# Windowed attention and a gated MLP on one core: V's scale through DRAM, and a pair's ten scores in one PE group

## The chip, the cores and the metric

One core of a Trainium2 chip runs the whole program: TensorE (PE), VectorE (DVE), ScalarE (ACT), GpSimd (POOL) and SyncE (SP), whose queue issues every transfer of this kernel. The metric is the device time of one execution in microseconds. Before the change the median of three runs is 649.65 us (648.05 to 651.03).

## The reference

Eight batches, eight heads, 576 positions, head dimension 64. Attention looks back over a window of 128 positions with a linear bias per head, and its output (8 x 64 = 512 channels) goes through a gated MLP with a spatial product.

```python
scores = scale * np.matmul(q, k.transpose(0, 1, 3, 2))
mask = (rel >= 0) & (rel < window)                  # window = 128
scores = np.where(mask, scores + bias[None], -1000000000.0)
attn = softmax(scores)                              # max taken off, sum + 1e-09
x = np.matmul(attn, v)                              # heads side by side: 512 channels

h = np.maximum(x @ w_in, 0.0)                       # 1024 channels: u and v
v_n = (v - mean(v)) / np.sqrt(var(v) + 1e-06)
v_s = np.einsum('ts,bsd->btd', w_spatial, v_n) + b_spatial[None, :, None]
out = (u * v_s) @ w_out
```

## The kernel before

**Attention.** Two heads make a pair, with 64 partitions each, so a batch has four pairs. The 576 queries of a pair are five tiles (four of 128, tile 4 of 64), and a tile of queries sees the keys of its own and of the tile before: 128, 256, 256, 256 and 192 columns. A pair goes through these steps, in `attention` (line 498 on):

- scores (L520): ten f32 matmuls in the 64-row shape, the two heads side by side in the array. They come in two PE groups (`PIECES`): tiles 0 to 3 in four PSUM banks with the tag `s`, and tile 4 in two banks of the same tag. A profile shows each f32 matmul as two records, so the groups are 16 and 4 records.
- DVE adds the bias and takes the row maximum (L531), ACT takes the exponential with its row sum (L537), ACT and DVE normalise into a high and a low f16 part, `pq` (L557, L562), and two transfers of SP transpose `pq` into `pt` (L568).
- V's scale: V is split into two f16 parts, which needs a power of two near the largest magnitude of the pair. ACT takes the sum of magnitudes of each partition into column 0 of `am` (L579); PE turns that column into a row (L583, in a bank with the tag `x`); DVE takes the maximum (L587, L588); two PE matmuls against constants bring it back to all 128 partitions, times 2^-12 and 2^-13/4096 (L593); DVE keeps the exponent bits (L599, L600). Then follow `vh` (L604 or L607) and `vl` (L611).
- P times V (L624): 42 small f16 matmuls into both banks with the tag `x`; ACT and DVE scale and split the result into the pair's `xt` (L633, L637).

**The gated MLP** of a batch is made of units, each one PSUM bank with the tag `m` (there are two): five V units (L689; L711 for the last 64 rows) of 512 columns, then eight U units (L741), eight spatial units (L762) and eight output units (L788) of 288 columns. V and U units take the four pairs one after another, three matmuls for each; output units go over four `gs` tiles in the same way. Behind a spatial unit DVE multiplies (L770) and splits (L776); the results of output units go to `o` and are stored by SP (L798). The weights are f32r parts, so a unit has 12 to 14 matmuls.

**The order.** `Plan` collects each step with its engine, a weight, a due time and what it reads and writes; tiles with a tag form rings of so many buffers. It then lists the steps by a simulated clock: on each engine the ready step with the earliest due time comes next. The engines run these lists in order. The scores, V's scale and P times V of batch b's pairs are thereby woven into the units of batch b - 1. SP's list holds loads, transposes and stores, and a transfer that waits there holds up those behind it.

The first batch and pair 0 of the second take another way (`raw_tile`, L430 to L484), without V's scale; the other 27 pairs take the way above.

## Time and profile before

| what | value |
|---|---|
| median of three runs | 649.65 us |
| profiled execution, its own time | 648.05 us |
| its span, first to last instruction | 646.3 us |
| PE busy | 619.0 us (96%) |
| DVE busy | 524.2 us (81%) |
| ACT busy | 430.9 us (67%) |
| granted TensorE clock, mean | 0.992 |
| share of PE in the chain that ended last | 79% |
| transfers, mean | 123 GB/s |

The profile is of the run with 648.05 us; 1.75 us of it lie outside the span. Matmuls are pipelined, so that the durations of their records overlap: 12 matmuls of 288 columns have records of some 0.3 us each, and start 0.13 us apart. A row of the timeline has the start, the length up to the end of the last record, engine, line, operation, tiles and shapes, and the number of instructions that it merges. The tiles' names in the profile: `qkraw` holds q and k, `s`, `x` and `m` are PSUM banks, `am` the scale, `one` the maximum, `ident` and `ones` constants.

### The profile page before, as it was taken

The numbers are of one execution on the slowest core, as the hardware profiler recorded it, in microseconds if no ns is written. First come the engines' busy times: TensorE is split into PE (matmuls) and PEld (weight loads), VectorE is DVE, ScalarE is ACT, GpSimd is POOL, SyncE is SP. The second block draws the span as 40 slices with busy tenths as digits, with TensorE's granted clock in tenths as the row PEclk, the third lists the DMA queues.
The fourth block names the chain that finished last, engine by engine and source line by source line (L and its number), as shares of the span: only waits on it lengthen the run. The fifth ranks groups of instructions, "written<-read, shape, count | busy, mean of one in ns | idle before, by whom it ended". The sixth has DMA issues, their size and how long they took to land.

```text
span 646.3 us, 14141 instructions
## 1 busy us (share of the span) xinstructions
PE 619.0 (96%) x5037; PEld 529.8 (82%) x5037; DVE 524.2 (81%) x1897; ACT 430.9 (67%) x1322; POOL 29.6 (5%) x53
## 2 busy tenths in 40 slices
PE   4879999999999999999999999999999999999997
PEld 2445688778899879988898979988898978988997
DVE  6999898999887979887887979887887979873632
ACT  4698675989585848686686848676686857662211
POOL 1000010000200010000100010000100010000100
PEclk9998799999999999999999999999999999999999
DMA  7903013799156863778165753858166751733001
GB/s 264 329 20 130 19 62 119 169 209 202 55 132 133 190 107 93 155 155 184 40 143 127 191 112 89 154 152 188 32 154 125 193 113 10 132 79 76 2 20 55
DMA packets 149291, 79.34 MB, mean 123 GB/s; under 512 B 128610, under 2 KB 139874, under 8 KB 149220
## 3 DMA queue, kind: packets, MB, share of 16 engines
q1 hardware_dynamic: 149220, 78.44, 51.8%
q8 instruction: 39, 0.64, 0.4%
q14 instruction: 32, 0.26, 0.1%
HBM read 37.13 MB, written 9.44 MB: 72 GB/s over the span
## 4 chain that ended last, share of the span: by engine, by line
PE 79%; DVE 17%; issue 1%; DMA 1%; ACT 1%; SPq 1%; ACTq 0%; DVEq 0%
PE m L762 16%; PE m L741 16%; PE m L788 14%; PE m L689 13%; PE s L520 8%; PE x L624 6%; DVE pq L562 4%; PE m L711 2%; DVE prob L436 2%; DVE prob L531 2%; DVE gs L298 1%; DMA pt<-in_qk_dram 1%; DVE prob L450 1%; DVE u L770 1%; DVE o L267 1%
## 5 line engine op out<-in xcount | busy, mean ns | idle before, releaser
L537 ACT ACTIVATE prob<-prob,stat 128x128 f32<-128x128 f32 (+1 forms) x270 | 125.4, 466 | 13.6 <-DVE stat L531 12.4
L762 PE MATMUL m<-wsp,vn 128*128 128x288 f32 x768 | 124.3, 299 | 0.7 <-DVE u L770 0.7
L788 PE MATMUL m<-gs,wout 128*128 128x288 f32 x768 | 113.5, 301 | 0.3 <-DVE gs L776 0.2
L762 PEld LDWEIGHTS m<-wsp,vn 128*128 128x128 f32 x768 | 107.5, 188 | 6.7 <-issue 1.9
L557 ACT ACTIVATE pq<-prob,stat 128x128 f16<-128x128 f32 x270 | 103.1, 464 | 12.7 <-ACT prob L537 10.2
L741 PE MATMUL m<-xt,win 128*128 128x288 f32 x768 | 111.6, 298 | 0.0
L788 PEld LDWEIGHTS m<-gs,wout 128*128 128x128 f32 x768 | 103.3, 188 | 7.2 <-issue 1.7
L562 DVE SCALAR_TENSOR_TENSOR pq<-prob,stat,pq 128x128 f16<-128x128 f32 x270 | 104.0, 437 | 4.3 <-ACT pq L557 3.7
L741 PEld LDWEIGHTS m<-xt,win 128*128 128x128 f32 x768 | 103.9, 188 | 4.1 <-issue 2.3
L689 PE MATMUL m<-win,xt 128*128 128x512 f32 x384 | 93.5, 396 | 1.7 <-DVE o L267 1.7
L531 DVE CUSTOM_DVE_ANT_0 prob<-s,tab 128x128 f32<-128x128 f32 (+1 forms) x270 | 89.2, 376 | 2.6 <-PE s L520 2.1
L689 PEld LDWEIGHTS m<-win,xt 128*128 128x128 f32 x384 | 71.5, 189 | 18.2 <-DVE o L267 2.8
L520 PE MATMUL s<-qkraw 64*128 64x256 f32 (+2 forms) x540 | 66.5, 360 | 1.5 <-DVE stat L531 1.3
L770 DVE TENSOR_TENSOR u<-m,u 128x288 f32<-128x288 f32 x64 | 28.9, 451 | 34.2 <-PE m L762 34.2
L520 PEld LDWEIGHTS s<-qkraw 64*128 64x128 f32 (+1 forms) x540 | 42.0, 175 | 16.2 <-issue 9.0
L659 POOL TENSOR_TENSOR st<-st,nhalf 128x1 f32<-128x1 f32 (+1 forms) x40 | 25.6, 640 | 560.4 <-DVE st L655 548.0
L537 ACT ACTIVATION_READ_ACCUMULATOR prob<-prob,stat 128x1 f32 x270 | 50.6, 187 | 0.0
L267 ACT COPY o<-m 128x288 f32<-128x288 f32 x37 | 14.6, 395 | 46.2 <-PE m L788 45.9
L624 PE MATMUL x<-pt,vh 128*64 128x256 f16 (+6 forms) x756 | 41.7, 229 | 0.0
L271 ACT ACTIVATE vt<-m 128x512 f32<-128x512 f32 x31 | 18.5, 598 | 33.0 <-DVE st L654 16.1
L637 DVE SCALAR_TENSOR_TENSOR xt<-x,am,xt 128x288 fp32r<-128x288 f32 x54 | 26.2, 507 | 17.1 <-ACT xt L633 17.0
L624 PEld LDWEIGHTS <-vh 128*64 128x64 f16 x756 | 31.7, 110 | 5.8 <-issue 3.5
(132 smaller groups left out, 820.7 us busy)
## 6 DMA issues: line engine op xcount, KB each, us to landing
qkraw<-in_qk_dram SPq DMA_DIRECT2D x28, 576.0 KB, 3.9
out_dram<-o SPq DMA_DIRECT2D x64, 144.0 KB, 2.0
vraw<-in_v_dram SPq DMA_DIRECT2D x28, 320.0 KB, 2.9
vn<-in_w_in_dram SPq DMA_DIRECT2D x6, 512.0 KB, 7.1
pt<-in_w_out_dram SPq DMA_DIRECT2D x4, 512.0 KB, 4.5
gs<-in_w_spT_dram SPq DMA_DIRECT2D x4, 288.0 KB, 5.0
xt<-in_w_in_dram SPq DMA_DIRECT2D x2, 512.0 KB, 6.8
qkraw<-in_qk_dram SPq DMA_DIRECT2D x3, 320.0 KB, 8.3
```

The lines of the kernel that those rows point to most:

```text
L520: nc.tensor.matmul(sc[k][j]()[:m, i, :k1 - k0], raw()[rows, 0, t * P:t * P + m], raw()[rows, 1, k0:k1], start=True, stop=True)
L531: nc.vector.tensor_tensor_reduce(pt(), sc()[:m, i, :n], tabs[h]()[:m, c0:c0 + n], -0.125, 3e38, ALU.add, ALU.min, st()[:m, NM, j, t:t + 1])
L537: nc.scalar.activation(pt(), pt(), AF.Exp, bias=st()[:m, NM, j, t:t + 1], scale=-1.0, accum_out=st()[:m, SM, j, t:t + 1])
L557: nc.scalar.activation(pq[j]()[:m, 0, cs], prob[j]()[:m, cs], AF.Copy, scale=st()[:m, RC, j, t:t + 1])
L562: nc.vector.scalar_tensor_tensor(pq[j]()[:m, 1, cs], prob[j]()[:m, cs], st()[:m, RC, j, t:t + 1], pq[j]()[:m, 0, cs], ALU.mult, ALU.subtract)
L624: nc.tensor.matmul(xp()[j * D:(j + 1) * D, x0:x0 + n], l()[:, kt, j * D:(j + 1) * D], rhs[:, o:o + n], start=j not in seen, stop=False, sk ...
L637: nc.vector.scalar_tensor_tensor(xt()[:, S + R + hf * HS:S + R + (hf + 1) * HS], xp()[:, :HS], am()[:, 6:7], xt()[:, qs].bitcast(F32), ALU ...
L689: nc.tensor.matmul(pt(), xt[c]()[:, X0[a] + t * P:X0[a] + (t + 1) * P], win()[:, c, w, DH:DF], start=(n == 0), stop=(n == 3 * NC_ - 1))
L741: nc.tensor.matmul(pt()[:, :HS], win()[:, c, w, d * P:(d + 1) * P], xt[c]()[:, X0[a] + hf * HS:X0[a] + (hf + 1) * HS], start=(n == 0), sto ...
L762: nc.tensor.matmul(pt()[:, :HS], l, r, start=(n == 0), stop=(n == len(ops) - 1))
L770: nc.vector.tensor_tensor(u(), pt()[:, :HS], u(), ALU.mult)
L788: nc.tensor.matmul(pt()[:, :HS], wout()[:, d, w, e * P:(e + 1) * P], gs[d]()[:, a, :], start=(n == 0), stop=(n == 3 * ND - 1))
```

## The change

**V's scale.** The column of magnitudes is written by SP to a tile in DRAM (`row`, 128 numbers) and read back by SP into all 128 partitions (`wide`, the front of the tile that `vl` will fill). DVE takes the maximum of each partition's 128 numbers, clamps it, keeps the exponent and multiplies by two constants (`powers`). The PE transpose, the two broadcasting matmuls and their bank are gone.

**The scores.** A new function `products` takes a list of groups. From batch index 2 on (`WHOLE = 2`) all ten scores of a pair form one PE group; tiles 0 to 3 stay in the four `s` banks, and tile 4 takes the two `x` banks that P times V also uses. DVE's steps of tile 4 get the earliest due times of the ten. The three pairs of batch index 1 keep two groups and `s` banks.

**The program's order.** `scores` and `attention` are now two functions, and the scores of a pair are recorded ahead of V's scale and P times V of the pair before it (`AHEAD = 1`), which sets the order in the rings of `s` and `x`.

```diff
+    AHEAD = 1
+    WHOLE = 2
...
+    dram = ctx.enter_context(tc.tile_pool(name="dram", bufs=2, space=bass.MemoryType.DRAM))
...
-    ones = fixed([1, 2 * P], BF16, "ones")
+    powers = fixed([P, 2], F32, "powers")
...
-    PIECES = (((0, 1), (2, 3)), ((4,),))
+    BANKS = (((0, 1), ("s", 4)), ((2, 3), ("s", 4)), ((4,), ("x", 2)))
...
+    def products(p, due, st, raw, RAWS, g, banks):
+        SM, NM, RC, TM = range(4)
+        sc = [[plan.buf(ps, *tag, [P, 2, 2 * P], F32) for _ in range(2)] for _, tag in banks]
+        span = [(k, i, t, min(P, S - t * P), max(0, (t - 1) * P), min(S, (t + 1) * P)) for k, (ts_, _) in enumerate(banks) for i, t in enumerate(ts_)]
+        def f():
+            for k, i, t, m, k0, k1 in span:
+                for j in range(2):
+                    rows = slice(j * D, (j + 1) * D)
+                    nc.tensor.matmul(sc[k][j]()[:m, i, :k1 - k0], raw()[rows, 0, t * P:t * P + m], raw()[rows, 1, k0:k1],
+                                     start=True, stop=True)
+        plan.add("PE", SWITCH + pe(*[4 * (x[5] - x[4]) for x in span]), due - 5000 + g * 3000, f, RAWS,
+                 [(sc[k][j], i) for k, i, *_ in span for j in range(2)])
...
+                d = due - 4500 + (t if len(banks) < 3 or t < NQ - 1 else -1) * 700 + j * 200
...
-        for g, banks in enumerate(PIECES):
+        for g, banks in enumerate((BANKS,) if b >= WHOLE else (BANKS[:2], ((BANKS[2][0], ("s", 4)),))):
+            products(p, due, st, raw, RAWS, g, banks)
...
+        return lambda: attention(p, due, vr, VRS, pts)
+    def attention(p, due, vr, VRS, pts):
...
-        def f():
-            nc.tensor.transpose(mp()[0:1, 0:P], am()[:, 0:1], ident())
-        def f():
-            nc.vector.tensor_reduce(one()[:, 0:1], mp()[0:1, 0:P], AX.X, ALU.max)
-            nc.vector.tensor_scalar(one()[:, 0:1], one()[:, 0:1], 2.0 ** -98, 2.0 ** 126, ALU.max, ALU.min)
-        def f():
-            for k in range(2):
-                nc.tensor.matmul(mp()[:, P + k:P + k + 1], ones()[:, k * P:(k + 1) * P], one()[:, 0:1], start=True, stop=True,
-                                 skip_group_check=True)
+        row = plan.buf(dram, "row", 2, [P, 1], F32)
+        wide = lambda: vl().rearrange("p a b -> p (a b)").bitcast(F32)[:, :P]
+        def f():
+            nc.sync.dma_start(row(), am()[:, 0:1])
+        plan.add("SP", 60, d + 1, f, [(am, 0)], [(row, 0)])
+        def f():
+            nc.sync.dma_start(wide(), row().rearrange("p o -> (p o)").partition_broadcast(P))
+        plan.add("SP", 300, d + 2, f, [(row, 0)], [(vl, 0)])
...
+            nc.vector.tensor_reduce(am()[:, 1:2], wide(), AX.X, ALU.max)
+            nc.vector.tensor_scalar(am()[:, 2:3], am()[:, 1:2], 2.0 ** -98, 2.0 ** 126, ALU.max, ALU.min)
+            nc.vector.tensor_scalar(am()[:, 2:3].bitcast(I32), am()[:, 2:3].bitcast(I32), bits, None, ALU.bitwise_and)
+            nc.vector.tensor_scalar(am()[:, 5:7], powers(), am()[:, 2:3], None, ALU.mult)
             nc.vector.tensor_scalar(am()[:, 5:6].bitcast(I32), am()[:, 5:6].bitcast(I32), bits, None, ALU.bitwise_xor)
...
+            todo.append((b, p, scores(b, p)))
+            if len(todo) > AHEAD:
+                rest(*todo.pop(0))
```

Where the order moves, three places matter. In the rows below, L numbers are those of the kernel that the rows are of; in the changed one the scores are L515, V units L700 and L722, U units L752, spatial units L773, output units L799 and P times V L635.

PE, in the middle of a batch, before: the scores of a pair, with U units.

```order
L689 MATMUL m<-win,xt 128x512 x24
L520 MATMUL s<-qkraw 128x128 x2
L520 MATMUL s<-qkraw 128x256 x6
L741 MATMUL m<-xt,win 128x288 x12
L583 MATMUL x<-ident,am 1x128
L741 MATMUL m<-xt,win 128x288 x12
L520 MATMUL s<-qkraw 64x192 x2
L593 LDWEIGHTS ones
L593 MATMUL x<-one,ones 128x1
```

PE at the same place with the change:

```order
L700 MATMUL m<-win,xt 128x512 x12
L722 MATMUL m<-win,xt 128x512 x8
L700 MATMUL m<-win,xt 128x512 x36
L515 MATMUL s<-qkraw 128x128 x2
L515 MATMUL s<-qkraw 128x256 x6
L515 MATMUL x<-qkraw 64x192 x2
L752 MATMUL m<-xt,win 128x288 x24
```

Tile 4's two matmuls stand directly behind the other eight and write to `x`; L583 and L593 are gone from between the units.

PE, at the turn from one batch's units to the next one's, before: the end of the batch's last P times V, two output units, and the first V unit.

```order
L624 MATMUL x<-pt,vl 64x64
L788 MATMUL m<-gs,wout 128x288 x24
L583 MATMUL x<-ident,am 1x128
L689 MATMUL m<-win,xt 128x512 x12
L593 LDWEIGHTS ones
L593 MATMUL x<-one,ones 128x1
```

PE at that turn with the change (the P times V is cut short):

```order
L515 MATMUL x<-qkraw 64x192 x2
L799 MATMUL m<-gs,wout 128x288 x48
L635 LDWEIGHTS vh
L635 MATMUL x<-pt,vh 64x256
...
L635 LDWEIGHTS vl
L635 MATMUL x<-pt,vl 64x64
L700 MATMUL m<-win,xt 128x512 x12
```

All four output units now stand ahead of P times V, and the first V unit directly behind it.

SP with the change, at the third scale that is made while a batch's units run (that of pair 0 of the next batch): `row` and `vl` are the two new transfers.

```order
L809 DMA out_dram<-o 128x288
L598 DMA row<-am 128x1
L809 DMA out_dram<-o 128x288
L602 DMA vl<-row 128x128
L578 DMA_TRANSPOSE pt<-pq_87 128x18x128
L578 DMA_TRANSPOSE pt<-pq_88 128x18x128
L414 DMA qkraw<-in_qk_dram 128x1152
```

DVE at the same scale with the change (L781 and L787 are the product and the split behind a spatial unit, L526 the maximum of scores):

```order
L781 TENSOR_TENSOR u<-m,u 128x288 x2
L607 TENSOR_REDUCE am<-vl 128x1
L608 TENSOR_SCALAR am<-am 128x1
L609 TENSOR_SCALAR am<-am 128x1
L610 TENSOR_SCALAR am<-powers,am 128x2
L611 TENSOR_SCALAR am<-am 128x1
L787 TENSOR_TENSOR gs<-u,gs 128x288 x2
L526 ISA prob_85,stat_89<-x,tab_71 64x192
```

On SP a pair's two transposes stand behind the second transfer, which waits for the first. On DVE the reduction, which waits for the second, stands between the products of the last two spatial units and their splits; behind these come the maxima of tile 4, which is the first tile that is read.

More of the change, by code (lines that the diff above doesn't have):

```diff
@@ L239, in f @@
             nc.vector.memset(ident(), 1.0)
-            nc.vector.memset(ones()[:, :P], 2.0 ** -12)
-            nc.vector.memset(ones()[:, P:], 2.0 ** -13 / PSC)
+            nc.vector.memset(powers()[:, 0:1], 2.0 ** -12)
+            nc.vector.memset(powers()[:, 1:2], 2.0 ** -13 / PSC)
             nc.vector.memset(nhalf(), -0.5)
             nc.vector.memset(rstat(), 1.0)
-        plan.add("DVE", dve(400), 500, f, (), [(ident, 0), (ones, 0), (nhalf, 0)] + [(rstat, k) for k in range(8)])
+        plan.add("DVE", dve(400), 500, f, (), [(ident, 0), (powers, 0), (nhalf, 0)] + [(rstat, k) for k in range(8)])
         def f():
@@ L492, in clear, with f @@
                      [k for a in range(2) for k in parts(pq[j], a * NB * P + OFF[NQ - 1], (a + 1) * NB * P)])
-    PIECES = (((0, 1), (2, 3)), ((4,),))
+    BANKS = (((0, 1), ("s", 4)), ((2, 3), ("s", 4)), ((4,), ("x", 2)))
     WINDOWS = (((0, 0, 256, 0), (1, 256, 160, 128), (2, 512, 32, 256)),
                ((1, 416, 96, 0), (2, 544, 224, 0), (3, 768, 192, 96), (4, 1024, 64, 224)))
-    def attention(b, p):
+    def products(p, due, st, raw, RAWS, g, banks):
[10 more added lines that the diff above has]
+                 [(sc[k][j], i) for k, i, *_ in span for j in range(2)])
+        for k, i, t, m, k0, k1 in span:
+            for j in range(2):
+                h, n, c0 = 2 * p + j, k1 - k0, P if t == 0 else 0
+                pt = lambda j=j, m=m, t=t, n=n: prob[j]()[:m, OFF[t]:OFF[t] + n]
+                d = due - 4500 + (t if len(banks) < 3 or t < NQ - 1 else -1) * 700 + j * 200
+                def f(sc=sc[k][j], pt=pt, i=i, j=j, h=h, t=t, m=m, n=n, c0=c0):
+                    nc.vector.tensor_tensor_reduce(pt(), sc()[:m, i, :n], tabs[h]()[:m, c0:c0 + n], -0.125, 3e38,
+                                                   ALU.add, ALU.min, st()[:m, NM, j, t:t + 1])
+                cols = parts(prob[j], OFF[t], OFF[t] + n)
+                plan.add("DVE", dve(n), d, f, [(sc[k][j], i), (tabs[h], 0)], cols + [(st, (NM, j, t))])
+                def f(pt=pt, j=j, t=t, m=m):
+                    nc.scalar.activation(pt(), pt(), AF.Exp, bias=st()[:m, NM, j, t:t + 1], scale=-1.0,
+                                         accum_out=st()[:m, SM, j, t:t + 1])
+                plan.add("ACT", act(n, 2), d, f, cols + [(st, (NM, j, t))], cols + [(st, (SM, j, t))])
@@ L502, in attention, with scores @@
+    def scores(b, p):
         due = FIRST + b * PERIOD - LEAD - (NP - 1 - p) * PERIOD // 4
@@ L510, in attention @@
                 raw_tile(b, p, t, raw, vr, xt, t % 4, due - 6000 + t * 1500)
[L511 to L539 removed]
+            return lambda: xt
+        for g, banks in enumerate((BANKS,) if b >= WHOLE else (BANKS[:2], ((BANKS[2][0], ("s", 4)),))):
+            products(p, due, st, raw, RAWS, g, banks)
         pts = []
@@ L830, in first, with rest @@
             win_weights(0, c, UDUE[c], w_u[c])
+    xts = []
+    def rest(b, p, f):
+        xts.append(f())
+        if p == NP - 1:
+            gated(b, [xts.pop(0) for _ in range(NP)])
     gated(0, x0, first)
+    todo = []
     for b in range(1, B):
-        xt = []
         for p in range(NP):
```

37 lines of the change are left out of this document (3 added, 34 removed).

## The prediction

> **What bounds the kernel now.** I read the page first (busy time, then the chain of work that ended last), and then three stretches of one batch each, from the first V unit (L689) of a batch to that of the next.
>
> ```profile
> PE 619.0 (96%) x5037; PEld 529.8 (82%) x5037; DVE 524.2 (81%) x1897; ACT 430.9 (67%) x1322; POOL 29.6 (5%) x53
> PE 79%; DVE 17%; issue 1%; DMA 1%; ACT 1%; SPq 1%; ACTq 0%; DVEq 0%
> 299.65:372.61 72.96, 72.53 (x620) 63.58 (x620) 61.04 (x224) 52.12 (x164) 3.17 (x5) 1.00 0.57 133
> 372.61:445.58 72.97, 72.53 (x620) 63.57 (x621) 61.04 (x224) 52.14 (x164) 3.17 (x5) 1.00 0.58 133
> ```
>
> In the last two rows the columns behind the length are PE, PEld, DVE, ACT and POOL, the granted clock, and the DMA share. A batch takes 72.96 us, PE is busy for 72.53 of it at full clock, DVE for 61.04. So PE sets the pace, and what is taken off PE is time, until DVE (11.9 us of slack) or a transfer steps in. A busy PE hides small losses, so I read the timeline from start to start: a block costs the distance from its first matmul to that of the next block.
>
> ```profile
> 314.74 1.79 PE L520 MATMUL s<-qkraw 64*128 64x128 f32 x16
> 316.46 1.85 PE L741 MATMUL m<-xt,win 128*128 128x288 f32 x12
> 318.16 0.27 PE L583 MATMUL x<-ident,am 128*1 128x128 f32 x1
> 318.18 1.84 PE L741 MATMUL m<-xt,win 128*128 128x288 f32 x12
> 319.96 0.54 PE L520 MATMUL s<-qkraw 64*64 64x192 f32 x4
> 320.43 0.20 PE L593 MATMUL x<-one,ones 1*128 1x1 bf16 x2
> ...
> 327.28 1.75 PE L741 MATMUL m<-xt,win 128*128 128x288 f32 x12
> 328.96 1.79 PE L520 MATMUL s<-qkraw 64*128 64x128 f32 x16
> 330.68 0.66 PE L762 MATMUL m<-wsp,vn 128*128 128x288 f32 x3
> ...
> 332.71 0.54 PE L520 MATMUL s<-qkraw 64*64 64x192 f32 x4
> 333.18 0.67 PE L762 MATMUL m<-wsp,vn 128*128 128x288 f32 x3
> ...
> 335.14 1.75 PE L741 MATMUL m<-xt,win 128*128 128x288 f32 x12
> 336.73 0.56 PE L762 MATMUL m<-wsp,vn 128*128 128x288 f32 x3
> ...
> 342.03 0.65 PE L762 MATMUL m<-wsp,vn 128*128 128x288 f32 x3
> ...
> 344.06 0.20 PE L593 MATMUL x<-one,ones 1*128 1x1 bf16 x2
> 344.19 1.86 PE L788 MATMUL m<-gs,wout 128*128 128x288 f32 x12
> 345.98 1.79 PE L520 MATMUL s<-qkraw 64*128 64x128 f32 x16
> ```
>
> The undisturbed unit is 335.14 to 336.73: 12 matmuls in 1.59 us, 0.1325 each, so 14 of L762 take 1.855. The same 12 take 1.68 ahead of scores (327.28 to 328.96): going into the 64-row shape costs 0.09.
>
> **What leaves PE.** The transpose of the maxima (L583): 318.18 to 319.96 is 1.78; less 1.59 and less 0.09 into the scores leaves 0.10, and its own step (318.16 to 318.18) is 0.02. I take **0.11 us**, far under the 0.27 of its record, which overlaps its neighbours.
>
> The two broadcasting matmuls (L593): the 14 matmuls from 342.03 to 344.06 take 2.03 instead of 1.855, of which 0.08 is the aftermath of a transpose just ahead and 0.09 the way in; their own step is 0.13 (344.06 to 344.19); the 12 behind them take 1.79 (344.19 to 345.98), 0.09 of it into scores and 0.11 aftermath. Together **0.33 us**. Behind tile 4's scores (319.96, 320.43) the way in and out is the scores' own, and only 0.13 goes; that is one pair in four.
>
> Tile 4's scores in a group of their own (332.71): the block ahead takes 2.03 (330.68 to 332.71), 0.09 of which is the way in; the block takes 0.47; the 14 behind it take 1.96 (333.18 to 335.14), 0.11 over: 0.67 in all. In the common group the work remains: the four tiles' 896 columns take 1.72 and these 192 take 0.47, so 1.78 ns per further column and 0.34 us. The merge saves **0.33 us**.
>
> [...]
>
> Two waits go with these instructions:
>
> ```profile
> 289.99 0.88 PE L520 MATMUL s<-qkraw 64*64 64x192 f32 x4
> 290.79 3.44 PE L788 MATMUL m<-gs,wout 128*128 128x288 f32 x24
> ...
> 298.94 0.27 PE L583 MATMUL x<-ident,am 128*1 128x128 f32 x1
> 299.65 0.73 PE L689 MATMUL m<-win,xt 128*128 128x512 f32 x2 [0.43 <-DVE o L267]
> ...
> 298.30 0.93 DVE L637 SCALAR_TENSOR_TENSOR xt<-x,am,xt 128x288 fp32r<-128x288 f32 x2
> 299.15 0.44 DVE L267 COPY o<-m 128x288 f32<-128x288 f32 x1
> ```
>
> Tile 4's group waits inside (0.80 to the next block, not 0.47): 0.33 once a batch from the third on (five times). And the first V unit starts 0.71 behind a transpose that costs 0.02 elsewhere: 0.68, four times (298.94, and at the same place of the next three batches), because its m bank is emptied by a DVE copy that stands behind the split of P times V. In the new order four output units and then P times V stand ahead of that V unit, so the bank it takes is emptied during P times V.
>
> **What moves, and what covers it.** At the batch's end P times V now stands directly ahead of the V units that need its pair.
>
> ```profile
> 304.69 2.91 PE L689 MATMUL m<-win,xt 128*128 128x512 f32 x12
> 307.53 0.41 PE L624 MATMUL x<-pt,vh 128*64 128x256 f16 x4
> ...
> 308.96 0.89 ACT L633 ACTIVATE xt<-x,am 128x288 fp32r<-128x288 f32 x2
> 309.04 5.78 PE L689 MATMUL m<-win,xt 128*128 128x512 f32 x24
> 309.70 0.50 DVE L637 SCALAR_TENSOR_TENSOR xt<-x,am,xt 128x288 fp32r<-128x288 f32 x1
> ```
>
> The first half of xt is there 310.20 - 309.04 = 1.16 us after PE is through with P times V. A V unit takes the pairs one after another, three matmuls each; the fourth pair is asked for by its tenth, after 9 x 0.237 (2.84 / 12) = 2.1 us. The cover holds by 0.9 us; gone, it costs up to 1.2 us a batch. In the same way a group of ten scores comes to tile 4, the one that waits for the x banks, 1.72 us after its start.
>
> **What is added.** DVE's five operations for four.
>
> ```profile
> L587 DVE TENSOR_REDUCE one<-x 1x1 bf16<-1x128 f32 x27 | 7.4, 273 | 0.0
> L599 DVE TENSOR_SCALAR am<-x 128x2 int32<-128x2 int32 x27 | 4.1, 154 | 12.3 <-PE x L593 12.3
> out_dram<-o SPq DMA_DIRECT2D x64, 144.0 KB, 2.0
> qkraw<-in_qk_dram SPq DMA_DIRECT2D x28, 576.0 KB, 3.9
> pt<-pq SPq DMA_TRANSPOSE x54, 4.7
> ```
>
> The reduction has the same 128 elements per partition (273 ns), the small ones 154 ns each; one more is 0.15 us a pair, 0.6 a batch, on an engine with 11.9 us to spare: nothing, as long as that slack lasts. SP issues two more transfers per pair, in a row: the second waits on SP for the first to land, and pq's transposes, loads and stores queue behind it. No row shows so small a transfer. From below it is the store of o, 2.0 us; from above a transpose, 4.7, if it runs into one; I take 2.0 to 2.5, nearest to the store, so 4 to 5 us from the maxima to DVE's reduction. DVE waits there only if the transfers are later than the order assumes; today it waits for PE at the same place, 12.3 us in all (the row of L599), without PE standing still for it.
>
> **The sum**, against the profiled execution's own 648.05 us (span 646.3 and 1.75 around it; the median of the runs shown is 649.65, 1.6 above):
> - transposes 27 x 0.11 = 3.0
> - broadcasts 20 x 0.33 + 7 x 0.13 = 7.5
> - merges, 24 pairs, 24 x 0.33 = 7.9
> - waits that go: about 4 x 0.68 and 5 x 0.33 = 4.4
>
> That is 22.8 us. New waits: DVE would be busy 61.7 of some 69.1 us, and the batch gets denser around two m banks.
>
> ```profile
> DVE am L599 <- PE x L593: 2.3, 2, 2.2
> ```
>
> From below they cost 0; from above 2.3 us a batch, as if all that DVE waits for the broadcast in the batch from 299.65 on (this row of its waits: 2.3 us in 2 waits) came out at PE. I take 0.7, nearer to 0 since the two covers hold in the rows; six batches make 4.2 us. The start, where PE waits for several things at once, I leave as it is. 648.05 - 22.8 + 4.2 = 629.5; the profiled execution being the fastest of its runs, I forecast **630**.
>
> **The rivals.**
>
> *DVE becomes the bound* (faster, by less). For: 84% busy, 89% in the shorter batch, and in-order. Against: its waits today are mostly for PE, and shrink with it. If its idle time falls only from 11.9 to 9.5 us, a batch takes 61.7 + 9.5 = 71.2: six batches gain 10.6, with the first batch's pairs (3 x 0.44 = 1.3) 12 us: 636.
>
> *The shared x banks couple two pairs* (faster, by less). P times V cannot start before tile 4 of the next pair's scores is read, nor these scores' last tile before ACT and DVE have emptied P times V. Against: in DVE's new order the two reads of tile 4 come first of the ten, and the 1.72 us above. If each of 24 groups waits 0.4 us, 9.6 us come back: 639.
>
> *The scale comes late and DVE stands still* (slower). One place: the scale behind the last spatial unit, where DVE has the reduction between two u products and the two gs splits that the next output units need. From the pair's Abs on ACT to there PE has three spatial units, 5.6 us, less the Abs itself; I estimate 5 us for both transfers. At 3.9 each, like the load of q and k, they take 7.8 and DVE waits 2.8 us; the scores (2.06) and nine matmuls (1.19) cover 3.25, but DVE's own 2.7 there (4 x 0.45, 0.9) use most of it: PE loses 2.3. At two of a batch's four scales, 14 in all, that is 32 us and 657. It decides from 22.8 / 27 = 0.84 us of lost PE per pair on. Against it: at the other places the order has more between them. [...]
>
> *The gain is swallowed* (no change). The planner's new order opens holes that eat all 22.8 us, at the start above all: 646 to 651. The order shows ten scores in one group and no L583 or L593, so the work itself does go.
>
> **Chances.** Forecast (622 to 634) 0.62; DVE's bound 0.18; x banks 0.08; late scale 0.06; swallowed 0.06. A measurement of this kernel tells about 0.5% from no change, 3.2 us. Faster: 0.62 + 0.18 + 0.08 and a part of the last, 0.89; same 0.05; slower 0.06. The range takes in the first three: from 622 (no new waits, 625, and the start's holes smaller too) to 642.
>
> **What would show it.** Right: a batch from V unit to V unit of 69 to 70.5 us, PE busy for nearly all of it; 20 records of scores in about 2.05 us start to start; the first V unit right behind P times V without a gap over 0.3 us; DVE waiting for row and vl transfers under 1 us each. Wrong in the price of switches: a batch without waits that is longer than 69.5. Late scale: DVE's reduction at the top of the waits, released by a transfer, and gaps of PE in output units. DVE's bound: PE gaps released by DVE copies and u products, and DVE above 90%.

## The result, and the profile after

The changed kernel takes **811.71 us** (median of 4 runs, 809.56 to 813.86) against 649.65 us for the kernel before in the same comparison (median of three; a fourth execution of it took 1167.1 us and isn't counted): a ratio of 1.2496, 95% interval 1.2438 to 1.2554. The forecast was 630. The page of the changed kernel, its first rows and the chain of work that ended last:

```profile
span 807.8 us, 14073 instructions
PE 657.9 (81%) x4956; PEld 573.0 (71%) x4956; DVE 530.9 (66%) x1922; ACT 437.4 (54%) x1324; POOL 30.0 (4%) x53
PEclk9988996979998789888898798988988999989999
PE 14%; DMA 7%; DVE 2%; ACT 2%; SPq 0%; issue 0%; ACTq 0%; DVEq 0%
```

81 instructions have left PE (5037 to 4956), and yet its records take 38.9 us more in all, since the granted clock falls (mean 0.898, before 0.992). DVE's busy time has hardly moved (524.2 to 530.9). No engine is near its limit. The chain could be followed back only to 595.25 us, so its shares can't be set beside those of before; of the 212.5 us that it covers, the 7% of DMA, nearly all of it the two new transfers, are some 59. Two batches in the middle, in the columns that the prediction explains:

```profile
376.94:472.87 95.93, 78.18 (x610) 70.29 (x608) 62.32 (x227) 52.88 (x163) 3.29 (x5) 0.88 0.53 100
472.87:568.95 96.08, 77.44 (x609) 69.48 (x608) 62.41 (x228) 52.89 (x163) 3.29 (x5) 0.89 0.54 102
```

A batch takes 96 us instead of 73. PE is idle for 18 of them, and its 610 instructions take 78 us. What was waited for, from the table of waits (engine, what it wanted to do, the releaser; us in total, times, longest), the third row from the same table of SP's queue; below them the reduction's row among the costliest groups:

```profile
DVE am L607 <- DMA vl<-row: 142.8, 26, 10.1
PE m L773 <- DVE u L781: 41.6, 7, 6.8
SPq L602 <- DMA row<-am: 156.9, 26, 8.4
L607 DVE TENSOR_REDUCE am<-vl 128x1 f32<-128x128 f32 x27 | 7.7, 286 | 142.8 <-DMA vl<-row 142.8
```

26 of the 27 reductions find their data missing, for 5.5 us in the mean. Before, DVE waited at this place for PE, 12.3 us in all. The rows of the transfers (size, then median us from issue to landing):

```profile
out_dram<-o SPq DMA_DIRECT2D x64, 144.0 KB, 4.0
vl<-row SPq DMA_DIRECT2D x27, 64.0 KB, 4.9
pt<-pq SPq DMA_TRANSPOSE x54, 5.4
row<-am SPq DMA_DIRECT2D x27, 0.5 KB, 8.8
```

The store of 512 bytes is the slowest of them, 8.8 us; the read takes 4.9. Together that is 13.7 us, where the prediction had 4 to 5. Stores of o are later too, 4.0 instead of 2.0. Such a median counts only transfers whose landing the profile can pair with their issue, and in the changed kernel these are few: 28 of the 64 stores of o, 9 of the 27 new stores and 13 of the 54 transposes. Where each transfer's completions are counted up to the next issue on the same semaphore, the store of o has 3.7 against 2.0 and the new store 8.5, but the transposes have 4.7 in both kernels; their 5.4 shows no delay.

One pair, from the timelines of SP, DVE and PE:

```profile
201.88 0.38 SPq L598 DMA_DIRECT2D row<-am  x1
209.03 0.32 SPq L602 DMA_DIRECT2D vl<-row  x1
209.44 6.85 SPq L578 DMA_TRANSPOSE pt<-pq  x2
...
213.38 0.29 DVE L607 TENSOR_REDUCE am<-vl 128x1 f32<-128x128 f32 x1 [4.73 <-DMA vl<-row]
216.07 0.45 DVE L781 TENSOR_TENSOR u<-m,u 128x288 f32<-128x288 f32 x1
...
210.22 1.74 PE L752 MATMUL m<-xt,win 128*128 128x288 f32 x12
216.57 0.97 PE L773 MATMUL m<-wsp,vn 128*128 128x288 f32 x3 [4.61 <-DVE u L781]
217.82 2.80 PE L773 MATMUL m<-wsp,vn 128*128 128x288 f32 x12
220.45 0.42 PE L773 MATMUL m<-r,l 128*128 128x288 f32 x2
```

SP stands behind its store from 201.88 to 209.03, DVE behind the read until 213.38. Queued behind DVE's reduction are the first steps of the next scores and then a u product; it is done at 216.52, and only then does PE, which ran out of work at 211.96, have an m bank. The clock is the second loss: behind the gap 12 matmuls take 2.63 us (217.82 to 220.45) instead of 1.59. Granted clock in that stretch, the sixth value behind the length:

```profile
216.57:220.71 4.14, 4.14 (x19) 4.14 (x20) 2.94 (x11) 4.01 (x17) 0.00 (x0) 0.59 0.97 260
```

### The profile page after: what moved, and what is told of

It reads as the page before. It is cut to its first block, busy times and chain, and to the rows that moved or that the text cites. A ratio compares the mean times of both kernels' runs of the same rounds, so it can differ in the third digit from the quotient of the medians.

```text
span 807.8 us, 14073 instructions
## 1 busy us (share of the span) xinstructions
PE 657.9 (81%) x4956; PEld 573.0 (71%) x4956; DVE 530.9 (66%) x1922; ACT 437.4 (54%) x1324; POOL 30.0 (4%) x53
## 5 line engine op out<-in xcount | busy, mean ns | idle before, releaser
L773 PE MATMUL m<-wsp,vn 128*128 128x288 f32 x768 | 138.3, 327 | 63.5 <-DVE u L781 41.6
L773 PEld LDWEIGHTS m<-wsp,vn 128*128 128x128 f32 x768 | 123.2, 215 | 67.7 <-DVE u L781 43.5
L799 PE MATMUL m<-gs,wout 128*128 128x288 f32 x768 | 126.2, 325 | 22.1 <-DVE gs L787 18.7
L532 ACT ACTIVATE prob<-prob,stat 128x256 f32<-128x256 f32 (+2 forms) x270 | 125.4, 467 | 33.7 <-DVE stat L526 33.5
L752 PE MATMUL m<-xt,win 128*128 128x288 f32 x768 | 119.4, 309 | 25.6 <-ACT vt L276 24.6
L799 PEld LDWEIGHTS m<-gs,wout 128*128 128x128 f32 x768 | 118.5, 214 | 28.7 <-DVE gs L787 20.3
L752 PEld LDWEIGHTS m<-xt,win 128*128 128x128 f32 x768 | 109.9, 198 | 31.6 <-ACT vt L276 25.8
L607 DVE TENSOR_REDUCE am<-vl 128x1 f32<-128x128 f32 x27 | 7.7, 286 | 142.8 <-DMA vl<-row 142.8
L700 PE MATMUL m<-win,xt 128*128 128x512 f32 x384 | 94.3, 401 | 5.9 <-DVE o L272 5.9
L700 PEld LDWEIGHTS m<-win,xt 128*128 128x128 f32 x384 | 73.4, 193 | 22.6 <-DVE o L272 6.1
L618 ACT ACTIVATE vh<-vraw,am 128x640 f16<-128x640 f32 x20 | 16.6, 828 | 133.7 <-DVE am L611 133.7
L526 DVE CUSTOM_DVE_ANT_0 prob<-s,tab 128x256 f32<-128x256 f32 (+2 forms) x222 | 75.6, 378 | 1.7 <-PE s L515 0.6
L781 DVE TENSOR_TENSOR u<-m,u 128x288 f32<-128x288 f32 x64 | 28.5, 451 | 43.2 <-PE m L773 43.1
L515 PE MATMUL s<-qkraw 64*128 64x256 f32 (+2 forms) x444 | 52.5, 371 | 3.0 <-DVE stat L526 3.0
L635 PE MATMUL x<-pt,vh 128*64 128x32 f16 (+6 forms) x756 | 46.8, 243 | 9.8 <-DVE stat L526 7.3
L532 ACT ACTIVATION_READ_ACCUMULATOR prob<-prob,stat 128x1 f32 (+1 forms) x270 | 51.1, 189 | 0.0
L635 PEld LDWEIGHTS <-vh 128*64 128x64 f16 x756 | 35.2, 118 | 15.6 <-issue 15.3
L515 PEld LDWEIGHTS s<-qkraw 64*128 64x128 f32 (+1 forms) x444 | 37.5, 190 | 12.2 <-issue 4.4
```

Source lines behind the costliest of these rows:

```text
L515: nc.tensor.matmul(sc[k][j]()[:m, i, :k1 - k0], raw()[rows, 0, t * P:t * P + m], raw()[rows, 1, k0:k1], start=True, stop=True)
L526: nc.vector.tensor_tensor_reduce(pt(), sc()[:m, i, :n], tabs[h]()[:m, c0:c0 + n], -0.125, 3e38, ALU.add, ALU.min, st()[:m, NM, j, t:t + 1])
L532: nc.scalar.activation(pt(), pt(), AF.Exp, bias=st()[:m, NM, j, t:t + 1], scale=-1.0, accum_out=st()[:m, SM, j, t:t + 1])
L635: nc.tensor.matmul(xp()[j * D:(j + 1) * D, x0:x0 + n], l()[:, kt, j * D:(j + 1) * D], rhs[:, o:o + n], start=j not in seen, stop=False, sk ...
L700: nc.tensor.matmul(pt(), xt[c]()[:, X0[a] + t * P:X0[a] + (t + 1) * P], win()[:, c, w, DH:DF], start=(n == 0), stop=(n == 3 * NC_ - 1))
L752: nc.tensor.matmul(pt()[:, :HS], win()[:, c, w, d * P:(d + 1) * P], xt[c]()[:, X0[a] + hf * HS:X0[a] + (hf + 1) * HS], start=(n == 0), sto ...
```

## The experiments

**The price of one small transfer.** The kernel before, with one more transfer per pair on SP's queue that nobody reads, in eight forms by turns.

```diff
+        kind = len(pairs) % 8
+        shape = ([P, 1], [P, 16], [P, P], [P, P], [1, P], [P, 1], [P, P], [P, P])[kind]
...
+            if kind == 0:
+                nc.sync.dma_start(to(), am()[:, 0:1])
+            elif kind == 1:
+                nc.sync.dma_start(to()[:, 0:1], am()[:, 0:1])
...
```

> The kernel before, with one extra small transfer per pair on SP that nothing reads, in eight forms by turns: the store of the column of maxima (128 x 4 B) packed into 512 B of DRAM, the same 64 B apart, the same 512 B apart, a store of 128 x 512 B, a store of 512 B from one partition, the column copied within SBUF (128 x 4 B), a broadcast read of 512 B into 128 partitions, a plain read of 128 x 512 B. Theory 1 (the late part is the confirmation of 128 writes into one short stretch of DRAM): the packed store lands after about 8 us, the spread stores and all others after 2 to 3 us. Theory 2 (4-byte writes to DRAM are slow wherever they go): all three 128 x 4 B stores take about 8 us, the 512-byte ones and the copy within SBUF 2 to 3. Theory 3 (the transfers of the changed kernel only waited in the rings behind other traffic): the packed store lands after 2 to 3 us here, as do all others. The time itself says little, since three forms hold up the f16 part of V.

651.0 us, beside 649.9 for the kernel before. The landing of each form, as the records of the trace's semaphores give it (issue to the last of its completions, 16 for all but the fifth form, which has 2; one value per transfer):

| form | us |
|---|---|
| 128 x 4 B into 512 B of DRAM (the change's store) | 8.6, 11.1, 8.75, 8.9 |
| 128 x 4 B, 64 B apart in DRAM | 7.2, 4.2, 4.2, 5.15 |
| 128 x 4 B, 512 B apart in DRAM | 4.2, 2.9, 1.9, 2.0 |
| 128 x 512 B to DRAM | 2.2, 4.55, 3.9 |
| 1 x 512 B to DRAM | 1.25 to 2.24 |
| 128 x 4 B within SBUF | 3.6, 4.8, 3.9 |
| 512 B of DRAM into all partitions | 3.2, 3.25, 3.3 |
| 128 x 512 B of DRAM into SBUF | 3.35, 3.6, 3.7 |

Neither the 512 bytes nor the 4-byte pieces make the store slow: 512 B apart the same pieces land in 1.9 to 4.2 us. Slow is to pack them into one stretch of 512 bytes: 8.6 to 11.1 us. Pieces 64 B apart lie between, 4.2 to 7.2; the one of 7.2 was issued 1.6 us behind a packed store. In the trace of the changed kernel, where no other 4-byte packets overlap them, the store's packets start 0.8 to 2.2 us after the issue and take 9 ns each; the 16 completions are spread out, mostly between 2 and 9 us. Why the shared stretch is slow no trace shows.

**Each half alone.** The merge and the new order, with V's scale left on PE; and the scale through DRAM alone, with the scores and the order of pairs as before.

```diff
 merge alone, against the changed kernel:
-            nc.sync.dma_start(row(), am()[:, 0:1])
-            nc.sync.dma_start(wide(), row().rearrange("p o -> (p o)").partition_broadcast(P))
+            nc.tensor.transpose(mp()[0:1, 0:P], am()[:, 0:1], ident())
...
 scale alone, against the changed kernel:
-    AHEAD = 1
-    WHOLE = 2
+    AHEAD = 0
+    WHOLE = 99
```

> The change without its scale: V's scale through PE as before, the ten scores of a pair in one group with tile 4 in the x banks, and the order with scores one pair ahead. Theory (PE sets the pace, a group of its own costs tile 4's scores 0.33 us, and the x banks' coupling is covered): 24 x 0.33 = 7.9 us and the wait of 0.33 inside five groups, 1.7, go, and some 1 to 2 come back: 641 us against 650, ratio 0.985 to 0.99. Rival (the x banks couple two pairs, and now three users share them): 650 to 660, with PE waits at the scores' records in x.

> The change without its merge: V's scale through DRAM, the scores in two groups and s banks and in the order of before. Theory (the two transfers take 8.8 and 4.9 us one after the other, and DVE, SP and then PE stand still behind them): 790 to 830 us, DVE's reduction waits for the transfer some 140 us in all. Rival (it takes the x banks and the new order to make the transfers late): under 700 us.

Merge alone: 648.03 us, ratio 0.9977 (0.9959 to 0.9994). Scale alone: 782.38, ratio 1.2070 (1.2006 to 1.2134). So the loss is the scale's; the order of the change makes it larger, 162 us over the kernel before instead of 133. Both expectations missed: the merge was to take 641 us, and the scale alone 790 to 830 with some 140 us of DVE's waits. The transfers of the scale alone, and DVE's waits for the read:

```profile
row<-am SPq DMA_DIRECT2D x27, 0.5 KB, 8.2
vl<-row SPq DMA_DIRECT2D x27, 64.0 KB, 4.9
...
DVE am L607 <- DMA vl<-row: 89.2, 22, 9.9
```

The merge alone gives less than its terms, because its order of pairs makes new waits: on the timeline of PE, P times V of one pair in each batch starts before `vl` is ready, and the U unit behind it waits for DVE.

```profile
320.43 0.41 PE L637 MATMUL x<-pt,vh 128*64 128x256 f16 x4
321.23 0.30 PE L637 MATMUL x<-pt,vl 128*64 128x256 f16 x2 [0.39 <-DVE vl L624]
...
323.46 0.79 PE L754 MATMUL m<-xt,win 128*128 128x288 f32 x4 [0.87 <-DVE u L276]
```

It is 3.03 us there from 320.43 to the next unit at 323.46, elsewhere 1.51. The ten scores take 2.19 us from start to start, 0.14 more than the predicted 2.05.

**The merge, with the scale's bank from the ring `s`** instead of `x`, on the guess that a third user of the x banks makes those waits:

```diff
-        mp = plan.buf(ps, "x", 2, [P, 512], F32)
+        mp = plan.buf(ps, "s", 4, [P, 512], F32)
```

> The merge alone with V's scale through PE, and the bank of that scale (the transposed maxima and the broadcast) taken from the four s banks instead of the two x banks. In the run of the merge alone P times V of one pair per batch stood still for 1.5 us within its 42 matmuls, where the scale's bank was a third user of the x banks. Theory (it is that third user): the gap goes, 6 x 1.5 = 9 us less than 648: about 639 us. Rival (it is tile 4's banks that P times V waits for): no change, 648.

664.48 us, ratio 1.0231 (1.0207 to 1.0256), where the guess gave 639. That place takes some 2 us instead of 3.03, but the scale's two PE steps and the U unit behind them lose 0.79, 1.25 and 1.14 us a batch, which then takes 75 us. So this run doesn't settle the guess; the kernel with a scale without transfers, further down, speaks against it.

**No transfer.** The changed kernel in its own order, without both transfers; the reduction takes a constant, so V's scale is left out.

```diff
-            nc.sync.dma_start(row(), am()[:, 0:1])
-            nc.sync.dma_start(wide(), row().rearrange("p o -> (p o)").partition_broadcast(P))
-            nc.vector.tensor_reduce(am()[:, 1:2], wide(), AX.X, ALU.max)
+            nc.vector.tensor_reduce(am()[:, 1:2], ident(), AX.X, ALU.max)
```

> The changed kernel without both transfers, in the same order: DVE's reduction reads a constant tile. It leaves out V's own scale (a constant one is used). It shows what the rest of the change brings. By the prediction's sum: 625 to 634 us. With what the run of the merge alone showed in place of it (the block of ten scores takes 2.19 us, not 2.05, so a merge saves 0.20 and not 0.33: 24 x 0.13 = 3.1 us less): 630 to 640 us. Rival (the x banks stop P times V here too, 1.5 us a batch and more): 640 to 650.

636.91 us, ratio 0.9794 (0.9777 to 0.9811). One batch, and PE's wait at the first V unit of a batch:

```profile
302.53:372.77 70.24, 69.54 (x609) 62.77 (x608) 61.87 (x228) 52.69 (x164) 3.29 (x5) 1.00 0.61 138
...
PE m L700 <- DVE o L272: 3.6, 5, 0.8
```

All of the change but the two transfers works: 13.2 us faster than 650.09. The transfers cost 811.7 - 636.9 = **174.8 us**. (The kernels were measured in several comparisons, in which the kernel before lay between 648.3 and 650.1 us; a difference of 2 us across them says nothing.)

**The waits one by one.** Three kernels in the changed order. DVE's reduction takes a constant, with both transfers as they are. Or the read takes a row of the input V, so that it doesn't wait for the store, which is still made. Or the read goes to a tile that nobody uses and DVE takes a constant, so that SP alone waits for the store. In none of them is V's scale the pair's.

```diff
 DVE's reduction free:
-            nc.vector.tensor_reduce(am()[:, 1:2], wide(), AX.X, ALU.max)
+            nc.vector.tensor_reduce(am()[:, 1:2], ident(), AX.X, ALU.max)
...
 store not waited for:
-            nc.sync.dma_start(wide(), row().rearrange("p o -> (p o)").partition_broadcast(P))
+            nc.sync.dma_start(wide(), v[0, 0][0, 0, :].partition_broadcast(P))
...
 only SP waits:
-            nc.sync.dma_start(wide(), row().rearrange("p o -> (p o)").partition_broadcast(P))
+            nc.sync.dma_start(side(), row().rearrange("p o -> (p o)").partition_broadcast(P))
```

> The changed kernel, instruction for instruction, but DVE's reduction reads a constant tile instead of what the broadcast read brings: both transfers still run and SP still waits for the store, DVE waits for neither. It leaves out V's own scale (a constant one is used). Theory (DVE, an in-order engine, stands before its reduction, 143 us in all, and PE behind it): nearly all is back, 635 to 660 us. Rival (SP, held 157 us behind the store, lets transposes, loads and stores come late, and they stop PE by themselves): above 700 us.

> The changed kernel, but the broadcast read takes 512 B of the input in place of the stored maxima: the store runs and nobody waits for it, DVE still waits for the read. It leaves out V's own scale (the maximum of other numbers of V is used). Theory (the store takes 8.8 of 13.7 us, and the list of steps has room for some 5): 640 to 670 us, and DVE waits under 1.5 us per pair. Rival (3 to 5 us of the read are enough to stop DVE): above 700 us.

> The changed kernel, but the broadcast read lands in a tile of its own that nobody reads, and DVE's reduction reads a constant tile (in the run where only the reduction was freed, DVE still waited 82 us for the same transfer at the low part of V, which overwrites its target). It leaves out V's own scale (a constant one is used). SP still waits for the store. Theory A (what SP holds up behind the store is enough): 690 to 750 us, with PE and DVE waiting for transposes and for stores of o. Theory B (DVE's and ACT's wait for the scale is what stops PE; SP's hold is covered): 637 to 655 us.

| kernel | us | ratio |
|---|---|---|
| DVE's reduction free | 751.23 | 1.1559 (1.1527 to 1.1592) |
| store not waited for | 722.55 | 1.1118 (1.1093 to 1.1143) |
| only SP waits | 731.41 | 1.1263 (1.1228 to 1.1299) |

The first is no clean cut: the read lands in the front of `vl`, so DVE waits for it one step later, 81.9 us in all. Waits of the second and the third:

```profile
DVE am L607 <- DMA vl<-in_v_dram: 65.4, 25, 7.0
vl<-in_v_dram SPq DMA_DIRECT2D x27, 64.0 KB, 7.6
```

```profile
DVE o L272 <- DMA out_dram<-o: 54.3, 14, 7.5
PE x L635 <- DMA pt<-pq: 24.9, 11, 9.3
```

No single waiter holds the loss: each wait that is taken away leaves 70 to 100 us over the kernel before. In the second a read of the input, which waits for nothing, lands after 7.6 us when it stands behind the store (3.2 to 3.3 by itself, above). In the third DVE and PE wait for stores of o and transposes, which the change doesn't touch.

**Planned for.** The changed kernel, its order made as if the store took 6.6 us and the read 2.7 us more, with Abs, store and read due 12 us earlier.

```diff
-        plan.add("SP", 60, d + 1, f, [(am, 0)], [(row, 0)])
+        plan.add("SP", 60, d0 + 1, f, [(am, 0)], [(row, 0)], lag=6600)     # d0 = d - 12000, for Abs too
-        plan.add("SP", 300, d + 2, f, [(row, 0)], [(vl, 0)])
+        plan.add("SP", 300, d0 + 2, f, [(row, 0)], [(vl, 0)], lag=2700)
```

> The changed kernel, with the list of steps made for what the two transfers took: 6.6 and 2.7 us are added to the planner's delay of the store and of the broadcast read, and the sum of magnitudes and both transfers are due 12 us earlier. Theory (the work on PE is less by 22.8 us, and the time was lost because the reduction stood in DVE's list, and the read in SP's, 9 us too early): 625 to 640 us, DVE waits under 1 us per pair for the transfer. Rival (so small a store also holds up the transfers around it, or SP has no room for it): over 660 us, with SP still waiting for the store and the transposes late.

726.35 us, ratio 1.1173 (1.1120 to 1.1225). DVE's wait for the read is gone, and the expectation of 625 to 640 still fell; its rival, over 660 with the transposes late, came (6.1 us by the median of the page, 4.7 before). Waits of DVE and of SP's queue:

```profile
DVE o L273 <- DMA out_dram<-o: 40.1, 9, 10.2
SPq L604 <- DMA row<-am: 32.1, 6, 8.3
```

**POOL's queue** for both transfers, in the changed order:

```diff
-            nc.sync.dma_start(row(), am()[:, 0:1])
+            nc.gpsimd.dma_start(row(), am()[:, 0:1])
```

and the read likewise.

> The changed kernel with both transfers issued from POOL's queue instead of SP's, in the same places of the order. SP no longer waits for the store. Theory A (SP's hold is most of the loss): under 720 us. Theory C (the slow confirmation of the store delays every transfer that follows it on the same 16 engines, whoever issued it; in the run where nobody waited for the store, the read behind it took 7.6 us instead of 3.2): above 760 us, the transfers of SP still land late (stores of o 4 us instead of 2.0), and DVE waits as long as in the changed kernel.

801.32 us, ratio 1.2347 (1.2318 to 1.2376). SP no longer stands behind the store, but POOL does (95.3 us in 11 waits), the store is about as slow from here (8.1 us), the transposes of SP's queue land after 5.9 us by the median of the page, which counts only those that it can pair with their issue, and DVE still waits 105.5 us for the read (142.8 in the changed kernel). The stores of o, expected at 4 us, have 2.3:

```profile
pt<-pq SPq DMA_TRANSPOSE x54, 5.9
row<-am POOLq DMA_DIRECT2D x27, 0.5 KB, 8.1
...
DVE am L607 <- DMA vl<-row: 105.5, 22, 10.5
```

**The store alone, the read alone, and the store 512 B apart.** After these runs it was open how the loss divides between the slow confirmation, what it does to transfers behind it, and a wait for any read in this order. Four kernels: the kernel without transfers, with the packed store added that nobody reads or waits for (V's scale left out); the changed kernel without the store, the read taking a row of the input V (not the pair's scale); and the changed kernel with the store's 4-byte pieces 512 B apart, once in its own order and once planned for. In these two the read takes the first partition's sum alone, so the maximum over partitions is left out.

```diff
 512 B apart:
-            nc.sync.dma_start(row(), am()[:, 0:1])
+            nc.sync.dma_start(apart()[:, 0:1], am()[:, 0:1])               # apart: [P, P] in DRAM
-            nc.sync.dma_start(wide(), row().rearrange("p o -> (p o)").partition_broadcast(P))
+            nc.sync.dma_start(wide(), apart()[0:1, :].rearrange("o f -> (o f)").partition_broadcast(P))
```

> The order of the kernel without the two transfers (636.9), and the store of the 128 sums alone, which nobody waits for; there is no read, and the reduction takes a constant, so V's scale is left out. Theory (a slow store costs only through those who wait for it): 636 to 645, transposes 4.7 to 5.0 us and stores of o 2.0 to 2.4. Rival (each transfer behind it is confirmed late as well): transposes above 5.5 us or stores of o above 2.8, waits of DVE for out_dram<-o and of PE for pt<-pq as in the run in which SP alone waited, time above 655.

> The changed kernel without the store; the broadcast read takes a row of the input V, and DVE waits for it as in the changed kernel, so V's scale is not the pair's. Against the run with the store not awaited (722.6, read 7.6 us): theory (the store in front of it makes the read late) read 3.2 to 3.8 us, time 640 to 665. Rival (the read alone is late in this order, and DVE's wait for it is the price): read above 5 us, time above 700.

> The changed kernel in its own order; the 128 sums are stored 512 B apart (first column of a 128x128 tile in DRAM), and the read takes that tile's first row, so V's scale comes from the first partition's sum alone: a part of the computation is left out. Theory (the price is that 128 writes of 4 B go into one stretch of 512 B): the store is confirmed 2 to 4 us after its issue instead of 8.8 and the read lands in 3 to 4, so DVE waits for the read under 50 us in all instead of 143, and the time is 640 to 690. Rival (any two small transfers in a row on SP in this order cost this, wherever they write): store above 6 us, time above 722, the time of the run in which the store was not awaited.

> The store 512 B apart as in the run above (scale from the first partition alone), and the order made with 1.8 and 2.0 us more for the two transfers and with Abs, store and read due 12 us earlier. Theory (with a store that is confirmed early the order can cover both transfers): DVE's wait for the read under 10 us in all, time 636 to 650, near the kernel without transfers. Rival (moving the transfers on SP disturbs transposes and stores as it did with the packed store, 726): above 690.

| kernel | us | ratio |
|---|---|---|
| no transfer | 636.91 | 0.9794 (0.9777 to 0.9811) |
| read alone, DVE waits for it | 640.87 | 0.9878 (0.9852 to 0.9904) |
| store 512 B apart, then the read | 644.27 | 0.9933 (0.9907 to 0.9958) |
| store 512 B apart, planned for | 648.66 | 0.9991 (0.9973 to 1.0008) |
| packed store alone, nobody waits | 683.32 | 1.0549 (1.0516 to 1.0582) |
| packed store, only SP waits | 731.41 | 1.1263 (1.1228 to 1.1299) |
| packed store and read: the change | 811.71 | 1.2496 (1.2438 to 1.2554) |

With the pieces 512 B apart, and the same instructions in the same order (beside one transfer that fills the tile at the start), the changed kernel is **no longer slower** than before: it is 0.7% faster, a small gain that the interval still sets apart from none. Its transfers, a batch in the middle, and DVE's wait:

```profile
apart<-am SPq DMA_DIRECT2D x27, 0.5 KB, 2.0
vl<-apart SPq DMA_DIRECT2D x27, 64.0 KB, 2.9
...
377.69:448.21 70.52, 69.79 (x609) 62.82 (x608) 61.89 (x228) 52.67 (x163) 3.29 (x5) 1.00 0.64 139
...
DVE am L610 <- DMA vl<-apart: 8.8, 7, 2.9
```

So 811.7 - 644.3 = 167.4 of the 174.8 us hang on the addresses of the store; a prompt store and the read together cost 7.4. The read changes a little with it: it needs one stored piece instead of 128, and lands after 2.9 us instead of 4.9; no run has the read of all 128 behind a prompt store. The read by itself costs 4.0, the order covers it nearly everywhere (DVE waits for it 5.2 us in all, in four waits). It lands after 3.3 us there:

```profile
vl<-in_v_dram SPq DMA_DIRECT2D x27, 64.0 KB, 3.3
```

That is the kernel with the unawaited store (722.55, read 7.6) less that store: a packed store that nobody waits for makes the read behind it 4.3 us later and the kernel 81.7 us longer.

The packed store alone costs 46.4 us by the medians although nobody waits for it. Its five runs spread from 672.02 to 685.10 us, the two lowest, 672.02 and 678.82, below the interval in the table; so the cost is 35 to 48. The expectation had the theory that a slow store costs only through those who wait; it fell. On SP's timeline, in the chain of waits, and among the waits of that kernel:

```profile
593.41 0.53 SPq L598 DMA_DIRECT2D row<-am  x1
595.31 10.34 SPq L809 DMA_DIRECT2D out_dram<-o  x3
...
595.31 9.40 DMA out_dram<-o
...
DVE o L272 <- DMA out_dram<-o: 35.1, 10, 10.6
```

A store of o that is issued 1.9 us behind the packed store lands 9.4 us later, at 604.71; without the packed store the median is 2.1. Its own 128 packets of 1152 B have all ended within 1.4 us of the issue, so what is late is the confirmation and not the data. The first of its 16 completions comes 0.7 us after the last of the packed store's. DVE waits for it with the next copy of o, and has ten such waits in all; without the packed store there is none. The trace of the changed kernel shows the same: five stores of o that are issued 0.4 to 0.5 us behind the packed store (one at 350.98) land after 8.3 to 11.0 us, four of them with the 128 packets ended by 1.4. In these four the first completion comes 0.4 to 2.5 us before the packed store's last. So the slow confirmation reaches transfers behind the store; the traces show the lateness, not what orders the completions.

Planned for, the kernel with the prompt store has no wait at the reduction left:

```profile
L612 DVE TENSOR_REDUCE am<-vl 128x1 f32<-128x128 f32 x27 | 7.3, 271 | 0.0
```

It is still no faster than before: the other order loses more elsewhere than the 8.8 us of waits that it saves. Two batches take 144.2 us there instead of 141.0; which waits make that up wasn't worked out. That it came in within its expected 636 to 650 is no merit of the plan.

**A scale without transfers.** One matmul against a 128 x 128 constant gives every partition the sum over all partitions, times 2^-12; DVE reads it from PSUM. The scale is then a power of two near the sum, instead of near the maximum, of the 128 sums. Once with the merge and the new order, once on the kernel before.

```diff
-            nc.sync.dma_start(row(), am()[:, 0:1])
-            nc.sync.dma_start(wide(), row().rearrange("p o -> (p o)").partition_broadcast(P))
+            nc.tensor.matmul(mp()[:, 0:1], ones(), am()[:, 0:1], start=True, stop=True, skip_group_check=True)
-            nc.vector.tensor_reduce(am()[:, 1:2], wide(), AX.X, ALU.max)
-            nc.vector.tensor_scalar(am()[:, 2:3], am()[:, 1:2], 2.0 ** -98, 2.0 ** 126, ALU.max, ALU.min)
+            nc.vector.tensor_scalar(am()[:, 2:3], mp()[:, 0:1], 2.0 ** -110, 2.0 ** 114, ALU.max, ALU.min)
```

> The merge and the order of the change, with V's scale by one PE matmul and no transfer: a 128 x 128 tile of constants times the column gives every partition the sum of all 128 (in place of their maximum; both bound V's largest magnitude, and the scale is a power of two that is undone behind P times V). Transpose, broadcast and the single-partition reduction are gone. Theory (PE sets the pace; the run without transfers took 637 us, and the matmul has the array's full shape, so some 0.1 us): 637 to 643 us. Rival (its bank is a third user of the x banks, 1.5 us a batch as in the merge alone): 646 to 650.

> The kernel before with nothing changed but V's scale by that one matmul: the scores in two groups, s banks, the order of before. By the terms of the prediction's sum: broadcasts 7.5 us and, of the transposes' 3.0, some 1.5 go, and the wait of the first V unit behind the transpose, 0.68 four times, may go too: 638 to 642 us. Rival (another wait takes their place): 645 to 650.

With the merge **634.50 us, ratio 0.9777 (0.9758 to 0.9795)**, faster than both kernels and under the 637 to 643 expected; on the kernel before 642.12, ratio 0.9895 (0.9876 to 0.9913), at the upper edge of its 638 to 642. A batch of the first:

```profile
368.52:439.07 70.55, 70.55 (x617) 63.73 (x616) 63.62 (x234) 49.48 (x155) 2.78 (x5) 1.00 0.60 138
```

PE is busy for all of it: this comes near to the kernel that the prediction had in mind, without the transfers. The scale's bank is here again a third user of the x banks, and in the middle batches P times V takes 1.51 us in nearly every pair, 1.85 at most. So a third user need not make the wait of the merge alone; here it holds its bank for one step of PE instead of two with DVE between them.

## Why the prediction was wrong

**What bounds the kernel, and what leaves PE: right but for two terms.** Without the transfers a batch takes 70.24 us, within the 69 to 70.5 that the prediction named, and the kernel 13.2 us less than before. It had 22.8 less 4.2, 18.6.

Two terms of that sum were mis-sized. The merge had 0.33 us for each pair; the ten scores take 2.19 us, so it is 0.33 - 0.14 = about 0.2, or 4.6 for 24 pairs instead of 7.9. And the wait of the first V unit for DVE's copy of o was to go (4 x 0.68); 3.6 us in five waits are still there, since P times V ahead of it didn't cover the copy. That the prediction charged 0.7 per batch for new waits makes up for part of this by luck: it is the old wait, not a new one. Taken by the batch, transposes 0.44, broadcasts 1.12, merges 0.8 and tile 4's wait 0.33 make 2.69; measured are 72.96 - 70.24 = 2.72.

**The covers, as far as the runs show them: right.** In the kernel without transfers no V unit waits for `xt`, and the scores wait 2.9 us in all for an emptied bank, in the first batch. There the rival of the x banks didn't come, and neither did DVE's bound: the batch of 70.55 us, in the kernel with the scale by one matmul, has DVE at 63.62, 90%, and PE idle at no point.

**What is added: this is the step that failed.** "No row shows so small a transfer. From below it is the store of o, 2.0 us; from above a transpose, 4.7 ...; I take 2.0 to 2.5, nearest to the store". The store took 8.8 and the read 4.9. The store of o was the wrong neighbour: it moves 144 KB in runs of 1152 bytes, this one 128 pieces of 4 bytes into one stretch, and no row of the trace before had that form. The bound from above was no bound. Where the pieces are 512 B apart, the two take 2.0 and 2.9 us, close to what the prediction took, and the kernel is at 644: the step failed by the addresses, not by the count of bytes or transfers. Even with a prompt store the forecast would have been low by 14 us, mostly by the two terms above and the 7.4 us that two prompt transfers cost.

**Where the cost falls: named as a rival, priced too low.** "The scale comes late and DVE stands still" gave the mechanism (reduction at the top of DVE's waits, released by a transfer, PE without m banks) and also what would show it; those rows are the ones above, though the gaps stand at spatial units more than at output units. It took 3.9 us for each transfer, 14 of 27 scales, and 0.06 for its chance. At 13.7 us for both, the same working gives DVE 13.7 - 5 = 8.7 us of wait and PE 8.7 - 0.55 = about 8 at a late scale, where the change costs 174.8 / 27 = 6.5 in the mean of all.

What it missed altogether is that a slow store reaches those who don't use it. It counted the queue of SP behind the store, but held the durations of all other transfers fixed. The packed store alone, awaited by nobody, costs 35 to 48 us; with the read and SP's wait 94; with DVE's wait 175. Part of each is the clock, which the prediction left out as well (granted in the mean 0.965, 0.944 and 0.898 in these three, 0.987 without transfers): in the changed kernel PE is busy for 657.9 us with the same 4956 matmuls that take 605.5 without transfers, 52 us more, at a granted clock of 0.898 in the mean. How much of these 52 lies on the path and how much beside other waits wasn't separated.

## What to carry to other kernels

Price a transfer by its pieces and where they land, not by its bytes or by the nearest row of another form: 128 pieces of 4 B into one stretch of 512 B of DRAM took 8.8 us here, the same pieces 512 B apart 2.0. Where no row has that form, measure it in a side transfer that nobody waits for, and leave the bound open above until then. And ask of a slow store what is issued behind it: taking its waiters away (683 to 751 us), planning for it (726) or moving it to another queue (801) didn't take the cost away here, where the kernel without transfers takes 637.

## What the runs showed of the hardware that was not expected

- The packed store of 512 bytes is confirmed 7 to 11 us after its issue, although its packets start 0.8 to 2.2 us after it, where they can be told apart, and take 9 ns each. Why the completions are spread out so the trace doesn't show.
- Transfers behind it are confirmed late: a read 7.6 us instead of 3.3, a store of o 9.4 instead of 2.1, with its data through after 1.4. With the store on POOL's queue, those transposes of SP's that the profile can pair with their landing have a median of 5.9 instead of 4.8, the stores of o 2.3 instead of 2.1; how far the lateness crosses queues isn't settled by that.
- After 4.6 us without work PE ran at a granted clock of 0.59 for 4.1 us, with 12 matmuls in 2.63 us instead of 1.59, so that this stall of DVE cost PE twice. In that kernel's trace 29 of the 30 stretches at a granted clock of 0.5 begin inside a gap of PE or up to 1 us behind it, and last 3.41, 6.83 or 10.24 us. That idling is the cause of the lower clock is read from this order; no run took it apart.
